# Three loads of a decode kernel get their last columns from compact copies that lie in 8, 4 and 2 shares

## The chip, the cores and the metric

The kernel runs on one core of a Trainium2 chip. The metric is the device time of one execution in microseconds; of several runs the median is given. The core has a tensor engine (PE, with its weight loads as PEld), a vector engine (DVE), a scalar engine (ACT), GpSimd (POOL) and SyncE (SP), which here issues nearly all transfers. Transfers are carried out by sixteen DMA engines, which work through what SP has queued.

## The reference

One token of each of four sequences goes through four layers: attention, MLP, and the same two again with the same weights and caches.

```python
def _A_ref(x, k_cache, v_cache, wq, wo):          # B=4, D=640, 32 heads of 128, window W=1024
    q = (x @ wq).reshape(B, 1, 32, 128) ...
    scores = jnp.einsum("bhqd,bhkd->bhqk", q, k) * (Dh ** -0.5)
    p = _softmax(scores, axis=-1)
    o = jnp.einsum("bhqk,bhkd->bhqd", p, v)
    return o.reshape(B, 1, 32 * 128) @ wo
def _B_ref(x, w1, w2):                            # 640 -> 1728 -> 640
    return relu(x @ w1) @ w2
x = x + _A_ref(_layernorm(x), ...); x = x + _B_ref(_layernorm(x), ...)
x = x + _A_ref(_layernorm(x), ...); x = x + _B_ref(_layernorm(x), ...)
```

All is float32. Keys and values of the window are 4 x 32 x 1024 x 128 numbers each, 134 MB together; they don't fit on the core and are read from DRAM in each of the two attention layers.

## The kernel before

The host lays the data of each head out as one *record*: 128 partitions (rows) of REC = 9472 columns, 37888 bytes a row. A row holds 640 columns of the query weights, 4096 of keys, 4096 of values and, from column WO = 8832 to the end, 640 of the output weights. The 32 records lie in DRAM behind one another in the tensor `rec`.

There are five slots of a record's size in the on-chip memory, and a sixth buffer, `ring`, a little smaller. Round one (the first attention layer) goes through records 0 to 31 in order; record h goes to slot h mod 5. The last six records of round one are kept on chip and are the first ones of round two. Between the rounds the MLP's weights pass through the ring.

For each record PE computes the query (5 matmuls of 128x4), the scores (8 matmuls of 4x512), the weighted values (8 of 16x512) and the projection by the output weights (4 matmuls of 4x160, one for each 160 columns of the last 640); DVE and ACT do the softmax between. The output projection is the last to read a record, one record's time after its scores.

All loads stand in one list, `items`, in the order in which they are wanted. `pump` takes them from its head as long as the columns that they overwrite are free, and issues them on SP's queue; `done` marks columns as read and calls `pump`. Each load has its own semaphore out of a set of eight that are used in turn. On the chip SP waits, for each load, until PE has read what is overwritten, and until the load that had the same semaphore before has landed; PE waits for a load's semaphore before its first reader. The function `cols` finds the columns that a matmul reads in the piece that brought them, so a reader's columns must lie in one piece.

Most records of round one come in one load of 128 rows (lines 189 and 190). The first, and the last few, come in pieces. A load is issued by the one line `sp.dma_start(...)` in `pump` (in the profile all such lines are those of the helper, L84 and L87).

Of the kernel before, what the change touches and what calls it, by code (L numbers as in the profile page):

```python
# [38 lines left out]
P = 128  # L39
B, D, H, DH, W, FF = 4, 640, 32, 128, 1024, 1728  # L40
NB = 4
FD = D // NB
# [4 lines left out]
WQ, K, V, WO = 0, D, D + 4 * W, D + 8 * W  # L47
REC = 2 * D + 8 * W
# [10 lines left out]
SIXTH = H - NS - 1  # L59
RING = WO + 2 * FD  # L60
# [7 lines left out]
W1_SLOT = [[0, 1], [2], [3], [4]]  # L68
W2_SLOT = [22, 20, 8, 4]
LATE = 5  # L70


class InOrder:
# [18 lines left out]


@with_exitstack
def decode_kernel(ctx: ExitStack, tc: tile.TileContext, xf, rec, w1, w2, out):
    nc = tc.nc
    pe, dve, act, pool, sp = (InOrder(tc, e) for e in (nc.tensor, nc.vector, nc.scalar, nc.gpsimd, nc.sync))
    sb = ctx.enter_context(tc.tile_pool(name="sb", bufs=1))
# [10 lines left out]
    hT = scratch.rearrange("p (m j) -> p m j", j=32)  # L109
    oTs = sb.tile([P, LATE, B], F32, name="oTs")  # L110
    qT = sb.tile([P, B], F32, name="qT")
# [46 lines left out]
    def home(h, r):  # L158

        if h == SIXTH:  # L160
            return "ring"
        return h % NS if not r or h >= LAST else (h + LAST) % NS
# [5 lines left out]
    buffers = dict(enumerate(slot)) | {"ring": ring}  # L168

    def load(key, src, lo, hi, buf, col):  # L170
        items.append((key, src, lo, hi, buf, col))

    def piece(r, h, lo, hi, buf=None, col=None):
        load(("rec", r, h), rec[h], lo, hi, home(h, r) if buf is None else buf, lo if col is None else col)

    def ending(r, hs, late):
# [4 lines left out]
        if late:  # L181
            for h in hs[-1:] + hs[-LATE:-1]:
                piece(r, h, WO, REC)
# [3 lines left out]
    piece(0, hs[0], 0, V)  # L187
    piece(0, hs[0], V, REC)
    for h in hs[1:-3]:
        piece(0, h, 0, RING if h == SIXTH else WO if h >= H - LATE else REC)  # L190
    piece(0, SIXTH, RING, REC, "ring", 0)
    ending(0, hs, True)
    loaded = {"w1": 0, "w2": 0}
# [17 lines left out]
    n = 0  # L211
# [4 lines left out]
    def pump():  # L216

        while items:
            key, src, lo, hi, buf, col = items[0]
            if any(b == buf and x < col + hi - lo and col < y for b, x, y in live):  # L220
                return
            sp.dma_start(buffers[buf][:, col:col + hi - lo], src[:, lo:hi])
            live.append((buf, col, col + hi - lo))
            if key:
                at.setdefault(key, []).append((lo, hi, buf, col))
            items.pop(0)
# [20 lines left out]
    def done(key, lo, hi):  # L247

        if key[0] == "rec" and key[1] == 0 and key[2] >= LAST:
            return  # L250
        if key == ("rec", 0, SIXTH):
            hi = min(hi, HELD)
        for x, y, buf, col in pieces(key):
            a, b = col + max(lo, x) - x, col + min(hi, y) - x
            if a < b:
                free(buf, a, b)
        pump()
# [3 lines left out]
    def put_by():  # L261

        for col, a, b in held:
            dve.tensor_copy(hold[:, col:col + b - a], ring[:, a:b])
            free("ring", a, b)
        pump()
# [13 lines left out]
    def center(fill):  # L280

        x = acc[:, :FD]
        dve.tensor_reduce(sums, x, op=OP.add, axis=AX.X)
        if fill:
            busy(256)
        pe.matmul(o_ps[:, :B], sums.to_broadcast([P, P]), pick, start=True, stop=True)
        dve.transpose(xT, x)
        dve.scalar_tensor_tensor(blocks, o_ps[:, :B].unsqueeze(1).to_broadcast([P, KB, B]), -1.0 / D, blocks,
                                 op0=OP.mult, op1=OP.add)
        dve.tensor_tensor(spread[:, :KB * B].rearrange("p (k b) -> p k b", b=B), blocks, blocks, op=OP.mult)  # L290
        dve.tensor_reduce(squares, spread[:, :KB * B].rearrange("p (k b) -> p b k", b=B), op=OP.add, axis=AX.X)
# [112 lines left out]


    pump()
    pe.matmul(acc[:, :FD], ident, x_sb, start=True, stop=False, skip_group_check=True)
    for r in range(2):
        hs = order[r]
        late = LATE if r == 0 else 2  # L410
        center(r > 0)
# [5 lines left out]
        for n, h in enumerate(hs[:-2]):  # L417
            i = n - (H - late)
            s = (n + 1) % 2
# [71 lines left out]
```

## Time and profile before

| | |
|---|---|
| median of three runs | 719.93 us (717.66 to 720.21) |
| the profiled execution | 718.78 us |
| its span in the profile | 717.1 us |
| moved by the DMA engines | 302.21 MB, 421 GB/s over the span |
| busy share of PE, DVE, ACT | 72%, 50%, 13% |
| packets on SP's queue (q1) | 15264 |

The profile is of one execution. Its span is the time from the first to the last recorded event, 717.1 us; the device time of the same execution is 1.7 us longer, so a sum made in the profile's microseconds is set against 718.78. The page's part 2 cuts the span into 40 slices and gives busy shares in tenths and the transfer rate; part 3 gives the queues of the DMA engines: q1 is SP's, q10 is ACT's, q8 and q14 fetch instructions. A packet is one contiguous row of a load, or a semaphore's update. The profile doesn't name the DMA engine of a packet.

### The profile page before, as it was taken

What the parts mean: (1) busy time and instruction counts of PE and PEld (TensorE: products, weight loads), DVE (VectorE), ACT (ScalarE), POOL (GpSimd) and SP (SyncE); (2) the same over time, 40 slices, a digit from 0 to 9 for tenths busy, and PEclk for the clock granted to TensorE, in tenths of its full rate; (3) what the DMA queues carried; (4) which work ended last, traced back from release to release, by engine and by line L of the source; (5) the groups of instructions that cost most, each with busy time, mean ns of one, the idle gap of its engine ahead of it and who ended that gap; (6) DMA issues with size and microseconds to landing.
All of it is one profiled execution on the core that took longest, in us unless ns stands there. A gap on an engine that the chain in (4) does not pass through costs nothing.

```text
span 717.1 us, 8939 instructions
## 1 busy us (share of the span) xinstructions
PE 516.8 (72%) x3686; PEld 208.9 (29%) x3686; DVE 359.1 (50%) x1013; ACT 93.0 (13%) x145; POOL 1.1 (0%) x9
## 2 busy tenths in 40 slices
PE   4467756667686676857877998876857777666977
PEld 2132222313233232322223433332322322323323
DVE  3344545354455444545731677744545445444661
ACT  1201011010101101111200312201011010101111
POOL 0000000000000000000000000000000000000000
PEclk9977888687767777787899899977787578867797
DMA  9999999999999999999989999999999999999996
GB/s 377 435 435 434 435 428 430 436 434 433 430 430 434 435 432 435 431 427 424 424 345 333 409 434 428 444 425 434 436 433 436 422 431 436 438 434 418 429 426 286
DMA packets 15336, 302.21 MB, mean 421 GB/s; under 512 B 1712, under 2 KB 2240, under 8 KB 5312
## 3 DMA queue, kind: packets, MB, share of 16 engines
q1 hardware_dynamic: 15264, 301.64, 98.6%
q8 instruction: 29, 0.48, 0.2%
q14 instruction: 11, 0.09, 0.0%
q10 hardware_dynamic: 32, 0.01, 0.0%
HBM read 301.56 MB, written 0.08 MB: 421 GB/s over the span
## 4 chain that ended last, share of the span: by engine, by line
DMA 80%; PE 15%; DVE 3%; issue 1%; another core or an unknown queue 0%; DVEq 0%; SPq 0%
DMA slot<-rec 68%; PE sc_ps L87 8%; DMA ring<-rec 6%; PE o_ps L87 4%; DMA slot<-w 3%; PE acc L87 3%; DMA ring<-w 3%; DVE scratch L87 2%; DVE oTs L87 1%; DVE small L87 0%; DVE t_ps L87 0%; DVE ring L87 0%; DVE mrt L87 0%; DVE xT L87 0%
## 5 line engine op out<-in xcount | busy, mean ns | idle before, releaser
L87 PE MATMUL sc_ps<-xT,slot 128*128 128x4 f32 x620 | 99.5, 287 | 148.9 <-DMA slot<-rec 146.6
L87 PE MATMUL sc_ps<-slot,qT 128*4 128x512 f32 x992 | 197.1, 935 | 1.0 <-DVE qT L87 1.0
L87 PEld LDWEIGHTS sc_ps<-xT,slot 128*128 128x128 f32 x620 | 95.4, 238 | 203.7 <-issue 194.0
L87 ACT ACTIVATE sc_ps<-sc_ps,small 128x1024 f32<-128x1024 f32 (+1 forms) x68 | 76.6, 1127 | 551.4 <-DVE small L87 551.2
L87 PE MATMUL o_ps<-slot,scratch 128*16 128x512 f32 x960 | 132.9, 674 | 2.5 <-DVE scratch L87 1.6
L87 DVE TENSOR_REDUCE small<-sc_ps 128x1 f32<-128x1024 f32 x64 | 78.3, 1223 | 77.2 <-PE sc_ps L87 77.2
L87 DVE STREAM_TRANSPOSE t_ps<-sc_ps 128x512 f32<-128x512 f32 x128 | 93.2, 728 | 2.1
L87 DVE COPY qT<-sc_ps 128x4 f32<-128x4 f32 x64 | 10.2, 160 | 160.9 <-PE sc_ps L87 160.9
L87 PEld LDWEIGHTS o_ps<-slot,scratch 128*16 128x16 f32 x960 | 32.6, 118 | 127.4 <-issue 81.3
L87 DVE SCALAR_TENSOR_TENSOR scratch<-o_ps,of_block,scratch 128x128 f32<-128x128 f32 x186 | 65.2, 351 | 6.6
L87 PEld LDWEIGHTS sc_ps<-slot,qT 128*4 128x4 f32 x992 | 33.1, 115 | 83.1 <-issue 72.3
L87 PE MATMUL acc<-slot,oTs 128*4 128x160 f32 x496 | 36.9, 385 | 15.7 <-DVE oTs L87 15.7
L87 DVE TENSOR_SCALAR scratch<-o_ps,of_block 128x128 f32<-128x128 f32 x62 | 21.7, 350 | 32.1 <-PE o_ps L87 32.1
L87 PE MATMUL o_ps<-pick,scratch 128*128 128x4 f32 x124 | 28.4, 299 | 6.5 <-DVE scratch L87 6.5
L87 DVE TENSOR_TENSOR scratch<-t_ps,mrt 128x64 f32<-128x64 f32 x128 | 28.8, 225 | 4.7
L87 PEld LDWEIGHTS o_ps<-pick,scratch 128*128 128x128 f32 x124 | 25.2, 251 | 9.4 <-DVE scratch L87 8.5
L87 PE MATMUL sc_ps<-slot,small 128*1 128x512 f32 (+1 forms) x36 | 17.1, 568 | 0.0
L87 DVE COPY oTs<-o_ps 128x4 f32<-128x4 f32 x62 | 10.0, 162 | 14.0 <-PE o_ps L87 12.9
L87 DVE TENSOR_SCALAR mrt<-of_batch,small 128x4 f32<-128x4 f32 x64 | 14.7, 230 | 2.2
L87 DVE STREAM_TRANSPOSE scratch<-small 128x32 f32<-128x32 f32 x64 | 12.9, 202 | 1.6 <-ACT sc_ps L87 1.6
L87 PE MATMUL sc_ps<-ring,xT 128*4 128x432 f32 x80 | 10.0, 605 | 4.6 <-DMA ring<-w 3.0
L87 PEld LDWEIGHTS acc<-slot,oTs 128*4 128x4 f32 x496 | 7.0, 84 | 21.0 <-DVE oTs L87 20.9
(62 smaller groups left out, 116.3 us busy)
## 6 DMA issues: line engine op xcount, KB each, us to landing
slot<-rec SPq DMA_DIRECT2D x43, 4736.0 KB, 30.7
slot<-rec SPq DMA_DIRECT2D x17, 2368.0 KB, 19.8
slot<-rec SPq DMA_DIRECT2D x2, 4416.0 KB, 35.1
slot<-rec SPq DMA_DIRECT2D x7, 1024.0 KB, 7.7
ring<-w SPq DMA_DIRECT2D x8, 864.0 KB, 27.2
ring<-rec SPq DMA_DIRECT2D x1, 4576.0 KB, 41.9
slot<-rec SPq DMA_DIRECT2D x2, 2048.0 KB, 38.2
slot<-rec SPq DMA_DIRECT2D x3, 1344.0 KB
```

Of the source, the lines that this page charges most:

```text
L87: r = build(*args, **kwargs)
```

## The change

The table `SHARED` names three records of round one: 8, 16 and 24. Each keeps its one load for all but its last n columns, with n = 640, 320 and 160. The last n columns come in a load of their own behind it. Its source is a new tensor in DRAM, made by the host: s8, s4 and s2 hold the 128 x n numbers in the order of the partitions, cut into k = 8, 4 and 2 shares of 128/k rows. A share is followed by 32 numbers of zero, so that the shares don't touch. The source is then described by three counts: k shares, 128/k rows, n columns; the destination is 128 partitions of n columns, as ever. The numbers that arrive are the same.

```diff
+SHARED = {8: (8, 4 * FD), 16: (4, 2 * FD), 24: (2, FD)}
...
     for h in hs[1:-3]:
-        piece(0, h, 0, RING if h == SIXTH else WO if h >= H - LATE else REC)
+        if h in SHARED:
+            k, n = SHARED[h]
+            piece(0, h, 0, REC - n)
+            load(("rec", 0, h), {8: s8, 4: s4, 2: s2}[k][:, :P // k * n].rearrange("a (b c) -> a b c", c=n), REC - n, REC,
+                 home(h, 0), REC - n)
+        else:
+            piece(0, h, 0, RING if h == SIXTH else WO if h >= H - LATE else REC)
...
-            sp.dma_start(buffers[buf][:, col:col + hi - lo], src[:, lo:hi])
+            sp.dma_start(buffers[buf][:, col:col + hi - lo], src[:, lo:hi] if len(src.shape) == 2 else src)
...
+    for h, (k, n) in SHARED.items():
+        part = np.zeros((k, P // k * n + 32), rec.dtype)
+        part[:, :P // k * n] = rec[h][:, REC - n:].reshape(k, -1)
+        arrays[f"s{k}"] = part
```

FD is 160. The order on SP's queue at record 8, before; it goes to slot 3 (a row is an instruction, with destination, source, shape and the semaphores that it waits for; DMAHW are those of loads):

```order
L87 DMA slot2_72<-rec 128x9472 [waits DMAHW7_49,DMAHW4_49,PE_49]
L87 DMA slot3_73<-rec 128x9472 [waits DMAHW0_49,PE_49]
L87 DMA slot4_74<-rec 128x9472 [waits DMAHW1_49,PE_49]
L87 DMA slot0_70<-rec 128x9472 [waits DMAHW2_49,PE_49]
L87 DMA slot1_71<-rec 128x9472 [waits DMAHW3_49,PE_49]
```

And now:

```order
L88 DMA slot2_72<-rec 128x9472 [waits DMAHW7_49,DMAHW4_49,PE_49]
L88 DMA slot3_73<-rec 128x8832 [waits DMAHW0_49,PE_49]
L88 DMA slot3_73<-s8 128x1x640 [waits PE_49]
L88 DMA slot4_74<-rec 128x9472 [waits DMAHW1_49,PE_49]
L88 DMA slot0_70<-rec 128x9472 [waits DMAHW2_49,PE_49]
L88 DMA slot1_71<-rec 128x9472 [waits DMAHW3_49,PE_49]
```

The load of record 8 is 640 columns shorter, one load from s8 stands behind it, and the later loads keep their order. At records 16 and 24 it is the same with 320 columns of s4 and 160 of s2.

On PE, the rows around the projection of record 8 (slot 3), before:

```order
L87 MATMUL sc_ps0_76<-xT_61,slot0_70 128x4 [waits DMAHW7_49,Activation_49]
L87 MATMUL sc_ps0_76<-xT_61,slot0_70 128x4 x4
L87 MATMUL o_ps_79<-pick_67,scratch_62 128x4 [waits DVE_49]
L87 MATMUL acc_80<-slot3_73,oTs_63 4x160 [waits DVE_49]
L87 MATMUL acc_80<-slot3_73,oTs_63 4x160 x3
```

And now:

```order
L88 MATMUL sc_ps0_76<-xT_61,slot0_70 128x4 [waits DMAHW0_49,Activation_49]
L88 MATMUL sc_ps0_76<-xT_61,slot0_70 128x4 x4
L88 MATMUL o_ps_79<-pick_67,scratch_62 128x4 [waits DVE_49]
L88 MATMUL acc_80<-slot3_73,oTs_63 4x160 [waits DMAHW6_49,DVE_49]
L88 MATMUL acc_80<-slot3_73,oTs_63 4x160 x3
```

The first projection matmul of the record now waits for the added load too (DMAHW6); the order of PE's work is the same.

More of the change, by code (lines that the diff above doesn't have):

```diff
@@ L94, in decode_kernel @@
 @with_exitstack
-def decode_kernel(ctx: ExitStack, tc: tile.TileContext, xf, rec, w1, w2, out):
+def decode_kernel(ctx: ExitStack, tc: tile.TileContext, xf, rec, w1, w2, s8, s4, s2, out):
     nc = tc.nc
```

## The prediction

> **What bounds the kernel now.** I read the page's summary first, then the chain that ended last, then a table by stage, then the change of rounds, where one engine's lateness would have to come out.
>
> ```profile
> span 717.1 us, 8939 instructions
> ...
> DMA packets 15336, 302.21 MB, mean 421 GB/s; under 512 B 1712, under 2 KB 2240, under 8 KB 5312
> ...
> q1 hardware_dynamic: 15264, 301.64, 98.6%
> q8 instruction: 29, 0.48, 0.2%
> ...
> q10 hardware_dynamic: 32, 0.01, 0.0%
> ...
> DMA 80%; PE 15%; DVE 3%; issue 1%; another core or an unknown queue 0%; DVEq 0%; SPq 0%
> ```
>
> SP's queue, q1, keeps the sixteen DMA engines occupied for 98.6% of the span, and 80% of the chain is transfer. The kernel is a stream out of DRAM with two interruptions, which the table by stage shows (columns: stretch, length, busy time and count of PE, PEld, DVE, ACT, POOL, granted clock, DMA share, GB/s):
>
> ```profile
> 100.00:200.00 100.00, 67.58 (x468) 28.03 (x464) 48.09 (x134) 11.66 (x18) 0.00 (x0) 0.77 1.00 433
> 358.00:394.00 36.00, 28.07 (x270) 9.77 (x266) 9.21 (x34) 2.96 (x7) 0.00 (x0) 0.96 0.93 341
> 412.00:454.00 42.00, 37.27 (x326) 16.08 (x330) 33.26 (x97) 7.77 (x12) 0.00 (x0) 0.91 1.02 434
> 690.00:717.10 27.10, 19.54 (x214) 7.41 (x210) 9.87 (x33) 3.95 (x7) 0.00 (x0) 0.86 0.80 334
> ```
>
> At full stream the core takes 433 GB/s, which is 433/16 = 27.1 bytes per ns for one engine. In 358 to 394 us only 341 GB/s flow. There round one ends: the stream has to wait for the work on it. So there are two independent streams, and what the first loses before 358 us isn't made up by the second, which starts after the wait and runs at its ceiling.
>
> The change touches the first stream alone. Its end, from the chain in order of time (start, length, what) and from the instructions in order of time (start, length, engine, what, then the idle time before it and its releaser):
>
> ```profile
> 315.38 40.86 DMA slot<-rec
> ...
> 356.37 3.61 PE o_ps L87 x16
> 359.98 4.12 PE sc_ps L87 x18
> ...
> 369.65 5.98 DMA ring<-w
> ```
>
> ```profile
> 356.37 3.61 PE L87 MATMUL o_ps<-slot,scratch 128*16 128x512 f32 x16 [0.94 <-DMA slot<-rec]
> ```
>
> A load of the last records holds the chain for 40.86 us up to 356.37, and PE stands idle for 0.94 us until it has landed. From there to 369.65 it is PE and DVE, and the weights of the MLP follow. A load is complete when the last of its engines is done. So a late engine shifts 356.37, and with it everything behind, one for one; an early one can win 0.94 us at most.
>
> **How many engines a load uses.** Packets under 512 bytes on this page are semaphore packets, one for each engine that takes part (the 640-byte rows are counted under 2 KB). q1's 15264 packets are 106 transfers of 144, that is 128 rows and 16 semaphores. That makes 106 x 16 = 1696 of the 1712. The other 16 belong to q10, the four loads of x, which have four rows each: 32 packets, 16 rows and 16 semaphores, four to a load. So a load of 128 rows runs on sixteen engines, and one of four rows on four. In these rows source and destination have the same number of rows. In the changed loads they don't: 128 partitions take in a source whose outermost count is 8, 4 or 2. I take the smaller count to decide. [...]
>
> **The change part by part.** Three loads lose their last 640, 320 and 160 columns (2560, 1280, 640 bytes a row), and three small loads bring them. No byte is added. The prices of such rows come from the only short rows that run alone, the store of the result:
>
> ```profile
> DMA packets 144, 0.08 MB, mean 39 GB/s; under 512 B 16, under 2 KB 144, under 8 KB 144
> ...
> q1 hardware_dynamic: 144, 0.08, 12.5%
> ```
>
> This is the stretch from 715 to 717.1 us, so 12.5% of 16 x 2.1 us is 4.2 us for 128 rows of 640 bytes: 33 ns a row, semaphores included. At 27.1 bytes per ns the bytes alone take 23.6, so a row costs some 9 ns beside its bytes. Hence 2560 bytes take 94.5 + 9 = 104 ns and 1280 bytes 47 + 9 = 56 ns.
>
> - Taken away, on every engine: 8 rows each of 2560, 1280 and 640 bytes less, 8 x 4480 / 27.1 = 1.32 us.
> - Load with 8 shares: 128 rows on eight engines, 16 each, 16 x 104 ns = 1.66 us.
> - With 4 shares: 32 rows on each of four, 32 x 56 = 1.79 us.
> - With 2 shares: 64 rows on each of two, 64 x 33 = 2.11 us.
>
> If the sets lie inside each other, two engines get 5.56 - 1.32 = **+4.2 us**, two get 3.45 - 1.32 = **+2.1**, four +0.3, and eight lose 1.3. In a stream in which every engine always has a next packet, an engine keeps its lateness until the stream stops. Nothing hides it but the lead that the loaded engines have over the last one. There is such a lead: engines don't end together. The stretch from 364 to 372 us, in 40 slices of 0.2 us:
>
> ```profile
> DMA  9999979997999979944765445441443039918298
> ```
>
> From the 18th slice (367.4 us) the share is at four to seven tenths, and it reaches 0 in the 32nd (370.2): some engines are out of packets up to 2.8 us before others. Some of that comes from instruction packets, which fall on single engines (up to 358 us):
>
> ```profile
> DMA packets 5527, 153.57 MB, mean 429 GB/s; under 512 B 617, under 2 KB 761, under 8 KB 821
> ...
> q8 instruction: 12, 0.20, 0.2%
> ```
>
> 0.2% of 16 x 358 us over 12 packets is 0.95 us each. Which engines are behind the page doesn't tell. If the ends are scattered evenly over 2.8 us, the later of two engines is on average a third of that, 0.9 us, before the last: 4.2 - 0.9 = +3.3. If the last engine is itself one of the second pair, +2.1; one of the first pair, +4.2; if both loaded pairs are the earliest, 4.2 - 2.8 = +1.4. I take **+3.0**, a little under the middle.
>
> The rest costs nothing that shows. SP issues three more loads; one issue takes a third of a microsecond:
>
> ```profile
> 351.46 0.33 SPq L87 DMA_DIRECT2D slot<-rec  x1
> ```
>
> ```profile
> SPq L87 <- PE acc L87: 479.4, 53, 26.2
> ...
> slot<-rec SPq DMA_DIRECT2D x43, 4736.0 KB, 30.7
> ```
>
> SP waits 479.4 us for PE's projections, and a full record lands 30.7 us after its issue, nearly three records (4736 KB at 433 GB/s is 11.2 us) deep in the queue. Behind the added loads stand only loads with that much time; without this cover the three issues would cost 1.0 us. PE's added wait stands before the projection, record 16's and 24's before its later blocks; these rows land at most some 4 us behind the rest of the record, and the projection comes a whole record after its scores. If that cover went, the next query would be late by the same lag, which is in the sum already.
>
> The profiled execution took 718.78 us, 1.7 us around its span; with 3.0 it would take 721.8. The median of the runs is 719.93, so I forecast 719.93 + 3.0 = **722.9 us**.
>
> **Rivals.**
> 1. *The small loads also slow other engines, and are slowed by them* (clearly slower). A load confined to a few engines has them write partitions that other engines are writing at full rate. If two engines meet at one place and share its rate, a row's byte time doubles: 16 x 198 + 32 x 103 + 64 x 56 ns = 10.1 us, less 1.32 and the lead of 0.9 is +7.8; if half the rows meet, about +5.5, or 725.4. It decides the sign beyond 0.5% (3.6 us) as soon as the 5.56 us become 5.9 (less 1.32 and 0.9 is 3.6). For it: 27.1 bytes per ns is the same rate in every full stretch, so something is at its limit. Against it: no row shows two transfers slowing each other. [...]
> 2. *The lead covers it.* The last engine is one of the eight that lose 1.3 us, and the loaded pair is at least 4 us ahead of it. Then the time stays at 719.9. Against it: a spread of 2.8 us is too small. For it: earlier in the stream it may be larger than where it is seen.
> 3. *The shares don't confine anything*: the 128 partitions decide. Each engine then has 24 rows more at 9 ns, +0.2 us: 720.1. The rows with four on both sides can't exclude it.
> 4. *The sets don't lie inside each other.* If each load starts on other engines, the worst is one load's extra, 2.11 - 1.32 = +0.8: 720.7.
> 5. *Faster*: the last engine is relieved, and PE gets at most its 0.94 us back: 719.0.
>
> **How the numbers follow.** Forecast 0.46, rival 1 0.24, rival 2 0.11, rival 3 0.09, rival 4 0.07, rival 5 0.03. The forecast's own range is 1.4 to 4.2, so 721.3 to 724.1. For eight in ten I go from 719.2 (which leaves out part of rivals 2 and 5 and the scatter of a median whose runs went from 717.66 to 720.21) to 726.0 (above half-met rows, short of +7.8). A measurement tells 0.5%, 3.6 us, from no change: slower means above 723.5. That is about a third of the forecast (0.16) and nearly all of rival 1 (0.23), rounded to 0.40; faster, below 716.3, has 0.03 left from scatter; the rest, 0.57, is no change.
>
> **What would show it.** The number of packets under 512 bytes: 1712 + 8 + 4 + 2 = 1726 if the shares confine the loads, 1760 if not. The q1 packets: 15264 + 384 + 14. The idle 0.94 us of PE at the end of round one should grow by about 3 us, the stretch of low DMA share there should begin about as early but end some 3 us later, and everything behind should be shifted by it: the second stream should have its old length from the MLP's last load to the end. I am wrong if records before the shared loads land later too, if the added time arises in round two, or if the span grows by over 5 us (rows meet) or not at all (1726 packets and no shift: the lead covered it).

## The result, and the profile after

The changed kernel takes 724.2 us in the median of four runs (722.88 to 725.04) against 718.93 (717.66 to 720.21, four runs; the 719.93 of the prediction is the median of three of them) before: 1.0072 of the time, with a 95% interval of 1.0047 to 1.0096. That is 5.2 us more (3.4 to 6.9). The forecast was 3.0 us more, 722.9 us, with 719.2 to 726.0 as its range. By its own mark, 723.5 us, the change came out slower, to which it gave a chance of 0.40. The profiled execution of the changed kernel took 724.51 us.

From the summary of the changed kernel:

```profile
span 722.7 us, 8943 instructions
...
DMA packets 15734, 302.21 MB, mean 418 GB/s; under 512 B 1726, under 2 KB 2510, under 8 KB 5710
...
q1 hardware_dynamic: 15662, 301.64, 98.4%
```

1726 semaphore packets are 1712 + 8 + 4 + 2: the three small loads run on eight, four and two engines. q1's 15662 packets are 15264 + 384 rows + 14.

Where the time came from shows in the table by stage (columns as in the prediction). Each of the three stretches of 24 us holds one of the small loads. Before:

```profile
98.00:122.00 24.00, 16.65 (x116) 5.70 (x112) 12.08 (x34) 2.59 (x4) 0.00 (x0) 0.78 1.00 432
...
188.00:212.00 24.00, 18.03 (x112) 7.30 (x108) 11.32 (x32) 2.59 (x4) 0.00 (x0) 0.64 1.00 430
...
278.00:302.00 24.00, 18.66 (x120) 6.96 (x116) 12.23 (x34) 2.59 (x4) 0.00 (x0) 0.71 1.01 438
```

And after the change:

```profile
98.00:122.00 24.00, 16.72 (x112) 6.86 (x108) 11.13 (x32) 2.59 (x4) 0.00 (x0) 0.71 1.00 400
...
188.00:212.00 24.00, 14.65 (x100) 5.75 (x99) 10.73 (x30) 2.59 (x4) 0.00 (x0) 0.78 1.01 416
...
278.00:302.00 24.00, 17.01 (x106) 7.20 (x106) 12.03 (x34) 2.62 (x5) 0.00 (x0) 0.72 1.00 425
```

The DMA share, the last number but one, stays at 1.00: the engines are occupied all the time. Yet the rate falls, from 432 to 400 GB/s at the load of 8 shares. A mere redistribution of rows between engines would have left the mean rate nearly where it was. 24 us x 32/432 is 1.8 us lost by the mean engine there, 0.8 at the second and some 0.7 at the third (where the rows of before scatter from 430 to 438 between neighbouring stretches).

The records of the single packets say the same. Their durations, from the trace, of the rows that the three small loads bring:

```
bytes a row   rows   usual ns   median   mean   longest
2560           128        102      174    162       284
1280           128         55       55     63        98
 640           128         32       32     35        54
```

The rows of the big loads that were under way beside the 8 shares took 18.3 us longer in sum than the same sizes take elsewhere, 1.1 us for each of sixteen engines.

How it reaches the end: the first instruction of DVE behind the attention of round one, and the first behind its MLP (start, length, what). Before:

```profile
367.12 0.33 DVE L87 TENSOR_REDUCE small<-acc 128x1 f32<-128x160 f32 x1 [0.85 <-PE acc L87]
...
391.03 0.32 DVE L87 TENSOR_REDUCE small<-acc 128x1 f32<-128x160 f32 x1 [10.48 <-PE acc L87]
```

After:

```profile
371.40 0.33 DVE L88 TENSOR_REDUCE small<-acc 128x1 f32<-128x160 f32 x1 [0.85 <-PE acc L88]
...
395.87 0.33 DVE L88 TENSOR_REDUCE small<-acc 128x1 f32<-128x160 f32 x1 [10.68 <-PE acc L88]
```

Round one's attention ends 4.3 us later, its MLP 4.8. From there to the end of the span it is 326.1 us before and 326.8 after. So the loss is that of the first stream, as the prediction had it, and the second round neither adds to it nor makes it good. The chain at the end of round one isn't quite the one of before. Again a load holds it for 40 us, but the MLP's weights follow at once, where before PE and DVE stood between them from 356.37 to 369.65 us:

```profile
322.90 40.73 DMA slot<-rec
...
363.65 10.58 DMA ring<-w
```

### The profile page after: what moved, and what is told of

The parts are those of the page before. It is cut to its first block, busy times and chain, and to the rows that moved or that the text cites. A ratio compares the mean times of both kernels' runs of the same rounds, so it can differ in the third digit from the quotient of the medians.

```text
span 722.7 us, 8943 instructions
## 1 busy us (share of the span) xinstructions
PE 523.5 (72%) x3686; PEld 210.2 (29%) x3686; DVE 358.9 (50%) x1013; ACT 93.1 (13%) x145; POOL 1.1 (0%) x9
## 2 busy tenths in 40 slices
DMA packets 15734, 302.21 MB, mean 418 GB/s; under 512 B 1726, under 2 KB 2510, under 8 KB 5710
## 3 DMA queue, kind: packets, MB, share of 16 engines
q1 hardware_dynamic: 15662, 301.64, 98.4%
## 4 chain that ended last, share of the span: by engine, by line
DMA 79%; PE 16%; DVE 3%; issue 1%; another core or an unknown queue 1%; DVEq 0%; SPq 0%
DMA slot<-rec 73%; PE sc_ps L88 9%; PE o_ps L88 4%; DMA ring<-w 3%; DMA slot<-w 3%; PE acc L88 2%; DVE scratch L88 2%; DVE oTs L88 1%; DVE small L88 0%; DVE t_ps L88 0%; DVE ring L88 0%; DVE qT L88 0%; DVE mrt L88 0%; DVE xT L88 0%
## 5 line engine op out<-in xcount | busy, mean ns | idle before, releaser
L88 PE MATMUL o_ps<-slot,scratch 128*16 128x512 f32 x960 | 134.6, 682 | 2.4 <-DVE scratch L88 1.3
```

Source lines behind the costliest of these rows:

```text
L88: r = build(*args, **kwargs)
```

## The experiments

Two readings of the result stood against each other. By the *queue theory*, the forecast's, a small load makes its few engines late by its rows at their usual price, and no other engine notices. By the *meeting theory*, the first rival, its engines write partitions that other engines are writing too, and both are slowed; which partitions an engine writes is supposed by it, as no trace names the engine of a row. A third, the *source theory*, came up with the result: the small compact tensors are slow to read. Times are compared with runs of the kernel before on the same chip (medians 718.8 to 719.3 us). The microseconds behind a ratio are worked out from it and can differ from the difference of the medians by up to 1.1 us, which is given where it matters.

### The same small loads without gaps between the shares

```diff
-SHARED = {8: (8, 4 * FD), 16: (4, 2 * FD), 24: (2, FD)}
+SHARED = {8: (128, 4 * FD), 16: (128, 2 * FD), 24: (128, FD)}
...
-        part = np.zeros((k, P // k * n + 32), rec.dtype)
+        part = np.zeros((k, P // k * n + (32 if k < P else 0)), rec.dtype)
```

> The three small loads stay, and so do their compact sources; only the gaps between the shares are taken away, so that each source is 128 rows. Queue theory (as in the sum: the price is the extra rows on a few engines, each at its usual price): sixteen engines share the rows again, 24 rows more for each at 9 ns, +0.2 us against the kernel before, semaphore packets 1712 + 48 = 1760. Meeting theory (the rows of a confined load land where other engines write, and both are slowed): every engine is back on its usual partitions, so also +0.2. Source theory (the small compact source in DRAM is slow to read): it stays slow, +3 or more, and the rate around the first small load stays at 407 GB/s, as in the changed kernel, and not 428.

Measured: 1.0001 (0.998 to 1.0022), no change. Packets from the summary, then the rate at the first small load:

```profile
DMA packets 15768, 302.21 MB, mean 421 GB/s; under 512 B 1760, under 2 KB 2544, under 8 KB 5744
```

```profile
98.00:122.00 24.00, 16.45 (x108) 7.12 (x104) 11.67 (x32) 2.59 (x4) 0.00 (x0) 0.71 1.01 437
```

1760 semaphore packets: sixteen engines a load. All 384 short rows take their usual time in the trace (102, 55 and 32 ns, none longer). So three more loads, short rows and compact sources cost nothing that can be measured. What costs comes with the gap of 32 numbers: with it the three loads have 8, 4 and 2 semaphore packets (1712 + 14 = 1726), without it sixteen each (1712 + 48 = 1760). The source theory falls.

### Sixteen shares: nobody has more rows than another

```diff
-SHARED = {8: (8, 4 * FD), 16: (4, 2 * FD), 24: (2, FD)}
+SHARED = {8: (16, 4 * FD), 16: (16, 2 * FD), 24: (16, FD)}
```

> The three small loads with sixteen shares of 8 rows each, all with gaps. Queue theory: every engine has 8 rows of each load, nobody is late, +0.2 us against the kernel before. Meeting theory: an engine gets 8 neighbouring partitions, which it doesn't get in a load of 128 rows, so rows meet: the rate in 100 to 120 us falls below 428 GB/s, to 410 to 422, and the time rises by 0.5 to 2.5 us though all engines have the same number of rows. Source theory: as slow as the change, +3 or more.

Measured: 1.0046 (1.0019 to 1.0074), 3.3 us.

```profile
98.00:122.00 24.00, 13.87 (x100) 6.89 (x96) 9.16 (x28) 2.59 (x4) 0.00 (x0) 0.78 1.01 408
...
188.00:212.00 24.00, 18.44 (x124) 7.47 (x127) 12.34 (x36) 2.59 (x4) 0.00 (x0) 0.71 1.01 423
```

By the ratio the time rose by more than the 0.5 to 2.5 us expected (its interval reaches down to 1.4, and the medians differ by 2.2). The rate fell below the 410 to 422 GB/s expected, to 402 in the 100 to 120 us of the expectation, though sixteen engines take part in each load (1760 semaphore packets), which makes 8 rows for each. This is a loss without any overloaded engine, which the queue theory can't give.

The same in twelve records, and its control without gaps:

```diff
+SHARED = {h: (16, 4 * FD) for h in range(2, 25, 2)}     # control: 128 instead of 16, no gaps
```

> The last 640 columns of twelve records in one load each with 16 shares of 8 rows. No engine has more rows than another. Queue theory: +1 us. Meeting theory: the first such load (record 8, in the run with sixteen shares) cost some 1.6 us in the mean of all engines; twelve cost 16 to 21 us, and the rate over 40 to 345 us falls from 432 to some 408 GB/s.

> The control for the run with sixteen shares in twelve records: the same compact sources and the same loads of 128 rows, without gaps between shares. Both theories: 12 x 8 rows at 9 ns, +0.9 us, 0 to +2 us; the rate over 40 to 345 us within 2 GB/s of 432.

Measured: 1.031 (1.0284 to 1.0337), 22 us, with sixteen shares; 1.0012 (0.9996 to 1.0029), 0.9 us, without gaps. The rate over 40 to 345 us before, with sixteen shares, and without gaps:

```profile
40.00:345.00 305.00, 215.31 (x1447) 86.17 (x1447) 151.97 (x420) 35.61 (x55) 0.00 (x0) 0.76 1.00 432
```

```profile
40.00:345.00 305.00, 200.57 (x1324) 84.20 (x1320) 137.59 (x380) 32.39 (x50) 0.00 (x0) 0.75 1.00 407
```

```profile
40.00:345.00 305.00, 205.66 (x1447) 87.29 (x1440) 151.30 (x421) 36.28 (x56) 0.00 (x0) 0.78 1.00 431
```

The two kernels have the same loads, bytes and packets (17064 in both, 1904 of them of semaphores). They differ in the gaps of the sources and, by the meeting theory, in which engine carries which rows; the last section of experiments tells the two apart. 305 us x 25/432 is 17.7 us for twelve loads, 1.5 us each; the time says 22, 1.9 each, where 16 to 21 us were expected.

### One small load at a time

```diff
+SHARED = {8: (8, 4 * FD)}       # and, in kernels of their own, {16: (4, 2 * FD)} and {24: (2, FD)}
```

> Only record 8's last 640 columns come in 8 shares; the loads of records 16 and 24 are whole again. Queue theory: eight engines get 1.66 us and lose 0.76, +0.9 less their lead, so 0 to +0.9 us, and the rate around it is unchanged in the mean of all engines (some 425 GB/s in 100 to 120 us). Meeting theory: +1 to +2 us, the rate in 100 to 120 us is 407 GB/s as in the changed kernel.

> Only record 16's last 320 columns come in 4 shares. Queue theory: four engines get 1.8 us and lose 0.4, +1.4 less their lead of 0.9: 0 to +1.4 us, the rate in 188 to 212 us near 430 GB/s. Meeting theory: the rows took 63 ns on average in the changed kernel, so +1.6 us of lateness, and the streams lose 1.0 us in the mean of all engines (416 GB/s in 188 to 212 us): +1 to +2.6 us. With +3.5 for 8 shares alone and +0.2 for 2 shares alone, the three would then add up to the 5.3 us of the change.

> Only record 24's last 160 columns come in 2 shares. Queue theory (extra rows on few engines at their usual price): two engines get 64 rows, 2.1 us, and lose 0.2: +1.9 us less their lead over the last engine, so 0 to +1.9 us; the rate around it is unchanged. Meeting theory (rows land where other engines write): rows of 640 bytes took 35 ns on average in the changed kernel instead of 32, so hardly more: +0.3 to +2.2 us, and the rate in 278 to 302 us is 425 GB/s as there instead of 438.

Measured: 8 shares alone 1.0049 (1.003 to 1.0067), 3.5 us; 4 shares alone 1.0049 (1.0033 to 1.0064), 3.5 us; 2 shares alone 1.0003 (0.9985 to 1.0021), 0.2 us. The rates at the load, in this order:

```profile
98.00:122.00 24.00, 16.18 (x112) 6.62 (x108) 11.10 (x31) 2.59 (x4) 0.00 (x0) 0.71 0.99 400
```

```profile
188.00:212.00 24.00, 15.14 (x108) 6.42 (x104) 10.47 (x31) 2.59 (x4) 0.00 (x0) 0.78 1.02 422
```

```profile
278.00:302.00 24.00, 14.53 (x104) 6.40 (x96) 10.33 (x30) 2.59 (x4) 0.00 (x0) 0.78 1.01 430
```

The order is the opposite of the forecast's, in which the 2 shares were the dearest (2.11 us, 1.9 without what the shortened load saves) and the 8 shares the cheapest (1.66, or 0.9). By the ratios 8 and 4 shares cost more than even the meeting theory had given them (up to 2 and 2.6 us), and 2 shares 0.1 us less than it had, which the queue theory allows. The rates fit the meeting theory for 8 shares (407 GB/s in 100 to 120 us, as it said); for 4 shares 422 lies between the two (416 and 430), and for 2 shares 430 does (425 and 438). Most of the 8 shares' loss is in round one. DVE's first instruction behind the attention comes at 370.32 us instead of 367.12:

```profile
370.32 0.33 DVE L88 TENSOR_REDUCE small<-acc 128x1 f32<-128x160 f32 x1 [0.85 <-PE acc L88]
```

The three alone add up to 7.2 us, the three together cost 5.2. With intervals of 1 to 2 us on each this is no contradiction. The traces show the losses one by one, in the start of each record's query on PE, which waits for that record (us later than in the profile of before; the run without gaps shows the scatter, half a us):

```
query of record        9     12     13     17     21     24     25
the change           1.3    2.3    2.3    4.5    4.7    4.6    4.6
8 shares alone       1.0    1.9    1.9    1.9    2.1    1.7    1.7
4 shares alone      -0.2   -0.2   -0.2    1.8    2.0    1.6    1.6
2 shares alone      -0.2   -0.2   -0.2   -0.2   -0.2   -0.3    0.5
2 shares, 5 times    0.3    0.2    1.6    3.4    6.8    8.4   10.4
without gaps         0.1    0.1    0.1    0.1   -0.3   -0.5    0.5
```

The 8 shares (record 8) and the 4 shares (record 16) cost some 2 us each, alone and together, and the 2 shares (record 24) nothing in either. So by the traces the losses do add, and the 3.5 us of the two ratios are somewhat high, within their intervals (from 2.2 and 2.4 us). The medians differ by 2.45, 2.65 and 0.5 us, which adds up to 5.6.

### The load of 2 shares five times

```diff
+SHARED = {8: (2, FD), 12: (2, FD), 16: (2, FD), 20: (2, FD), 24: (2, FD)}
```

> The same load of 2 shares for five records (8, 12, 16, 20, 24). If the same two engines carry all of them and nothing lets them catch up within round one, lateness adds up: five times 1.9 to 2.1 us, less one lead of 0.9 to 2.8 us, +7 to +10 us against the kernel before, and +7.6 to +8.4 against the run with record 24 alone. If the engines changed from load to load, or caught up between records, it would be +0.5 to +3 us.

Measured: 1.0095 (1.006 to 1.0131), 6.8 us, where one such load cost 0.2. That is 1.65 us for each of four more, against 1.9 to 2.1 expected. In the table above the first of the five loads (record 8) leaves no mark, those of records 12, 16 and 24 cost 1.3 to 2.0 us each at the next query. So lateness does add up, as if on engines that stay the same and have a lead at first. This part of the queue theory holds. Not all of the time is lateness, though: behind record 20 the queries come 4.8 us later by record 22. There the rate dips, to 393 GB/s in 212 to 278 us. SP waited 24 us for PE, some engines ran out of packets (a DMA share of 0.73 in 236 to 242 us), and from then to 278 us the rows of 37888 bytes took up to 172 ns longer than their usual 1401, 4.1 us in sum for the mean engine, with no small load among them. Why was not followed up, so the 1.65 us isn't a clean price of lateness.

### Which partitions a confined load writes

First record 8's rows in four loads of 32 neighbouring partitions, each with 8 shares of 4 rows, instead of one load of 8 shares of 16:

```diff
+            if isinstance(src, list):
+                for p, part in enumerate(src):
+                    sp.dma_start(buffers[buf][32 * p:32 * p + 32, col:col + hi - lo], part)
```

> As the run with record 8 alone, but its 128 rows come in four loads of 32 neighbouring partitions, each in 8 shares of 4 rows. Eight engines again carry 16 rows each. Queue theory: the same as with one load of 8 shares, within 0.3 us, and rows at the same price. Meeting theory: the eight engines of one load now write eight different groups of 4 partitions at a time instead of crowding on the same ones, so rows take nearer to 104 ns than in one load, the rate in 100 to 120 us lies above 415 GB/s, and the time is 0.5 to 1 us below that with one load.

Measured: 1.0047 (1.0026 to 1.0067), 721.48 us; with one load it was 721.65. The rate, and the end of round one's attention:

```profile
98.00:122.00 24.00, 18.26 (x120) 6.66 (x116) 12.49 (x34) 2.59 (x4) 0.00 (x0) 0.71 1.01 421
```

```profile
368.41 0.33 DVE L88 TENSOR_REDUCE small<-acc 128x1 f32<-128x160 f32 x1 [0.85 <-PE acc L88]
```

The rate is 421 instead of 400 (414 instead of 407 in 100 to 120 us, just short of the 415 that the meeting theory asked for), and this profile's attention ends 1.9 us earlier than with one load. The first 96 of the 128 rows took 102 ns, the last 32 in time 173; the mean is 120 instead of 160, so rows are nearer to the usual price, as the meeting theory said. If the rows go in the order of their loads, and if these engines write partitions 0 to 63 in the big loads, as the mirror images below suggest, it should have lengthened those of partitions 64 to 95 too, and that they weren't is not explained. The median time isn't 0.5 to 1 us lower; it is the same within 0.2 us, as the queue theory said. A gain of that size lies within the intervals, so by the time alone this run decides nothing.

Then twelve records in two mirror images, and a third kernel for the part that both have in common (a pair in the lists is the first partition of a load and its source):

```diff
+FIRST = 0          # 2 in the mirror image
...
+            load(("rec", 0, h), [(32 * (p + FIRST), sh[i][k * p:k * p + k, :32 // k * n].rearrange("a (b c) -> a b c", c=n)) for p in range(2)] +
+                 [(64 - 32 * FIRST, pl[i])], REC - n, REC,
...
+            load(("rec", 0, h), [(0, pl[i, :64]), (64, pl[i, 64:])], REC - n, REC,     # the third kernel
```

> The last 640 columns of twelve records (2, 4 ... 24): partitions 0 to 63 in two loads of 32 partitions with 8 shares of 4 rows, partitions 64 to 127 in a plain load of 64 rows. Eight engines get 8 rows of shares and 4 plain ones, eight get 4 plain ones. In the run with record 8 in four such loads, the rows for partitions 0 to 63 came first and took the usual 102 ns. Queue theory: the eight engines are late by 12 rows at 102 ns less 0.75 us, 0.47 us a record, 5.7 us in all less the lead: +3 to +5.5 us. Meeting theory: the eight engines write the partitions that they write in a load of 128 rows, so nearly the same, +3 to +7 us (the plain 64 rows may meet).

> The mirror image of the run before it: partitions 64 to 127 come in the two loads of 8 shares, partitions 0 to 63 in the plain load of 64 rows. Every engine carries the same number of rows as there. Queue theory: the same time as there, within 1 us. Meeting theory: the eight engines now write where the other eight stream, a row takes up to twice 102 ns and the streams lose as much: 4 to 9 us slower than the mirror image, and a lower rate over 40 to 345 us.

> The last 640 columns of twelve records in two plain loads of 64 rows, partitions 0 to 63 and 64 to 127; no shares, sixteen engines in each load, the same number of rows for all. It gives what the plain half in the two mirror images cost. Queue theory: 16 more semaphores a record and 8 rows at 9 ns, +1 us or less. Meeting theory: sixteen engines write one half of the partitions, eight of them the half of the others; the run with partitions 0 to 63 in own shares cost +20 us, of which lateness explains 3 to 5.5, so one plain half costs 14 to 17 us and two 20 to 33.

Measured: partitions 0 to 63 in shares 1.0276 (1.0251 to 1.0302), 20 us; partitions 64 to 127 in shares 1.0585 (1.0562 to 1.0609), 42 us; two plain halves 1.0292 (1.0251 to 1.0333), 21 us. The rates over 40 to 345 us, in this order:

```profile
40.00:345.00 305.00, 208.32 (x1329) 87.02 (x1333) 138.38 (x384) 32.38 (x50) 0.00 (x0) 0.72 1.00 411
```

```profile
40.00:345.00 305.00, 198.81 (x1212) 86.28 (x1208) 126.59 (x349) 29.81 (x46) 0.00 (x0) 0.70 1.01 385
```

```profile
40.00:345.00 305.00, 199.64 (x1336) 82.72 (x1327) 139.09 (x382) 32.73 (x51) 0.00 (x0) 0.77 1.00 406
```

The mirror images have the same loads, the same rows for each engine and the same bytes (17257 packets in both, 2096 of them of semaphores), and they differ by 22 us. All that is exchanged is the half of the partitions that the confined loads write. That settles the queue theory as the whole account, which had them equal within 1 us. Nor is it the gaps in the sources: the mirror images have the same ones, and the two plain halves, which have none, lose as much as the first image. If meeting is the cause, the eight engines of these loads write partitions 0 to 63 in a load of 128 rows, as shares there cost less (20 us and 411 GB/s, against 42 us and 385). This is a reading of times and rates, which no trace shows directly.

Sizes were missed. The first image cost 20 us, not 3 to 7, and the difference was 22, not 4 to 9. Two plain halves cost 21, at the low end of 20 to 33. If both halves cost the same, one is some 10 us, and 10 remain for the own shares, twice what lateness (5.7 us less a lead) explains.

The packets' records show what kind of loss it is. The middle column adds up by how much all rows of the loads, big and short, took longer than usual in 30 to 345 us, in the mean of sixteen engines (0.5 us in the kernel before):

```
                            short rows, mean ns   rows longer, us an engine   time, us
0-63 in shares                    113                     16.0                  20
64-127 in shares                  148                     34.3                  42
two plain halves                  134                     18.8                  21
16 shares, twelve records         135                     18.4                  22
no gaps, twelve records           102                      0.5                   0.9
```

So in the first image too most of the 20 us goes with slowed rows, and not with the mere number of rows of eight engines. Its plain half then costs more than half of what two plain halves do, or its own shares slow others as well; which, was not separated.

## Why the prediction was right or wrong

**The bound** held. Two streams, and a loss in the first that the second doesn't make good: 326.1 and 326.8 us behind the MLP.

**How many engines** was right: 1726 packets. In these three loads the smaller of the two outermost counts decided, 8, 4 and 2 against 128. That small loads share their engines, which the forecast supposed, is borne out for loads of the same count by the five loads of 2 shares (6.8 us, where one cost 0.2). That the sets of 8, 4 and 2 lie inside each other, from which the forecast's +4.2 and +2.1 us are added up, no run shows; the traces show in its place some 2 us for the load of 8 shares, some 2 for that of 4 and nothing for that of 2.

**The sum failed at what a confined load costs**: "Load with 8 shares: 128 rows on eight engines, 16 each, 16 x 104 ns = 1.66 us". 104 ns, worked out from the store of the result, is right for such a row beside the full stream in a load with 128 source rows: 102 ns in the run without gaps. In 8 shares the same rows took 162 ns in the mean, 2.6 us for 16. And the sum had no term at all for the rows of the other loads, which lost 18.3 us beside the 8 shares, 1.1 us for each engine. So "four +0.3, and eight lose 1.3" isn't what happened. The load of 8 shares, the cheapest of the forecast, cost 3.5 us alone by the ratio and some 2 by the trace. The load of 4 shares cost the same. And the 2 shares, on which more than a third of the forecast's 5.56 us rested, cost 0.2: their rows were hardly longer (35 ns for 32). That the forecast's 3.0 us came near 5.2 was luck: two terms were too small, one too large.

**The lead** is the simplest account of the single load of 2 shares, which without one would have cost 1.9 us and cost 0.2 (-1.1 to 1.5). It would then be 0.4 us at least and 1.7 by the median, where 0.9 was taken. It doesn't carry over to the changed kernel: if the sets lay inside each other, the loads of records 8 and 16 would have used up the lead of these two engines, and yet the query of record 25 comes no later than that of record 24 (4.6 us both). On which engines the losses fell no trace shows.

**What hides the rest** held: splitting three loads, with three more issues on SP and a wait on PE, costs nothing that can be measured (1.0001, and 1.0012 for twelve).

**Rival 1** had what the traces show: *the small loads also slow other engines, and are slowed by them*. Its price for half-met rows, +5.5 us, was nearer than the forecast's, but its number is partly luck too: it lengthened the rows of all three small loads by half, where those of 8 shares took 162 ns for 102, of 4 shares 63 for 55 and of 2 shares 35 for 32, and it too put nothing on the other loads' rows. Its argument against itself, that no row shows two transfers slowing each other, says only that no load of the kernel before showed it. If each engine kept to partitions of its own in loads of 128 rows, that would account for it, and for the mirror images (20 against 42 us); no trace shows that they do. **Rivals 3 and 4** fall, the first with the packets, the second with the five loads of 2 shares, as far as loads of the same count go. Rival 2, the lead, fits the 2 shares alone, and rival 5 didn't come.

**The signs that were named**: the span grew by 5.6 us (717.1 to 722.7), and "over 5 us (rows meet)" was the prediction's own sign of being wrong. The idle 0.94 us of PE before the weighted values didn't grow by 3 us; it fell to 0.3. PE's waits at the end of round one did grow, in other places. The sum of the waits for a record before scores or queries, 300 us to the MLP, before and after:

```profile
PE sc_ps L87 <- DMA slot<-rec: 7.0, 2, 3.6
```

```profile
PE sc_ps L88 <- DMA slot<-rec: 11.9, 4, 3.3
```

The stretch of low DMA share should have begun about as early and ended some 3 us later, as it would if a few engines alone were late. It moved as a whole. Before, it goes from 367.4 us to 370.6 (the prediction's view of 364 to 372 us); after the change it begins at 371.6, in the 19th slice, and ends at 374.8. The stretch from 368 to 376 us, in 40 slices of 0.2 us:

```profile
DMA  9989959897999679874734021212011000992176
```

Wrong was that lateness would be the only trace. "I am wrong if records before the shared loads land later too" was the wrong place to look: the rate at the loads themselves told it.

## What to carry to other kernels

When the transfers set the time, look at the outermost count of both sides of every load: here a source in 8, 4 or 2 separate pieces confined the load to as many engines (1726 semaphore packets, 1760 with whole sources), and a gap of 32 numbers was enough. But an even number of rows for each engine wasn't enough either: twelve loads in sixteen shares of 8 rows cost 22 us. Beside a stream of loads of 128 rows, keep a load at all 128 partitions with as many rows in the source (twelve of them cost 0.9 us). Where a load broke this, the stream around it paid too (18.3 us in sum over the rows beside the 8 shares), and the price of a transfer that ran alone (33 ns for a row of 640 bytes) said nothing of that part.

## What was not expected of the hardware

Sixteen shares of 8 rows, on sixteen engines with the same work, cost 1.9 us a load (22 us for twelve), and 128 rows in two plain loads of 64 partitions are as dear (21 us for twelve pairs), while the DMA share stayed at 1.00 over 40 to 345 us. What such loads and the stream beside them share, so that both lose rate, no run shows.
